# Attention feeding a gated convolution on one core: the keys of the later batches by plain loads summed on VectorE, a new order of the work over a group's four steps, and a new beginning

## The chip, the core and the metric

The kernel runs on one core of a Trainium2 chip. TensorE (PE), VectorE (DVE), ScalarE (ACT) and GpSimd (POOL) compute; SyncE (SP) computes nothing, it issues transfers (DMAs), one after the other, in the order of the program. POOL can issue transfers of its own. All of them are carried by the core's 16 DMA engines. The metric is the device time of one execution in microseconds (us), smaller being better.

## The reference: what is computed

For each of 4 batches: 12288 queries of 128 channels; keys that are also the values, which are a 4 x 4 mean over a 384 x 32 grid, 768 keys, times a matrix; softmax attention; then a causal convolution over 5 positions as a gate, and two projections.

```python
kv_pool = kv.reshape(B, H // r, r, W // r, r, C).mean(axis=(2, 4))   # r = 4
k = v = kv_pool.reshape(B, -1, C) @ w_sr
s = scale * (q @ k.transpose(0, 2, 1))
a = np.exp(s - s.max(-1, keepdims=True))
a /= a.sum(-1, keepdims=True) + 1e-09
x = a @ v
# then, over the sequence, K = 5, xp = x with 4 zeros ahead:
gate_pre = sum(conv_w[k] * xp[:, k:k + S] for k in range(K))
out = ((1 / (1 + exp(-gate_pre))) * (x @ w_val)) @ w_out
```

## The kernel before

**Groups and steps.** Queries are worked in 96 groups of 512 (24 per batch), each in four *steps* of 128 queries, numbered j = 0 to 3. The loop over t = 4 x group + step writes out by hand, engine by engine, what is issued in each step; every engine takes its instructions in that order. Work on a group is spread over six groups' time: `cur` is the group whose scores are being exponentiated, `last`, `avg`, `xg`, `mg`, `og` are those 1, 2, 3, 4 and 5 groups back.

**A tile of scores.** `score` (L262) makes 128 x 768 scores for the next step, as three sums of high and low parts. There are three such score tiles in PSUM, two banks each; a tile is free again when `p_lo` has read it. `row_max` (L268, DVE), `expo` (L280, ACT, in place), `p_hi` (L327, ACT) and, one step later, `p_lo` (L331, DVE) turn it into a high and a low half in f16, in `hl`.

**The transposes.** The weights `hl` of two steps together go through one transposing DMA (L335) into `pt`. In step 2 it is issued for steps 0 and 1 (in this text the *early* transpose), in step 0 of the next group for steps 2 and 3 (the *late* one). Two groups later, `av` (L344) multiplies `pt` with the values in 18 matmuls of 512 columns, split over the four steps by `AV_CUTS` (6, 3, 3 and 6 of them), into one PSUM bank. Each needs both transposes.

**The sums of the softmax.** The reciprocal of the sums (L287, step 0) is turned by PE (L290) into the shared bank `m`, copied (L297, step 1), written to DRAM as `rd` (L298) and read back broadcast to 128 partitions as `rb` (L303, step 3).

**After the attention.** In step 3, `x` (L361, DVE) is `av` times `rb`. Then POOL makes the taps and sums of the convolution (L371, L380; the last tap on ACT, L369), PE the two projections (`m`, L400 and L410), with tanh, product and evacuation between them; `out` leaves in pairs of groups (L424).

**Transfers on SP**, in order, for a pair of groups: q of two groups (L233, 512 KB), late transpose, `out` (512 KB), rd, early transpose, `rb` (256 KB), late transpose, rd, early transpose, `rb`. q is loaded two groups ahead.

**The keys.** For the first batch they come in 16 pieces of 384 KB (L118), each summed by DVE over 4 x 4 (L123). For the other three, `setup_steps` issues one thing per group, from the second group of the batch before: row 0 of each half of the grid by a plain load on SP (L131, 768 KB), then rows 1, 2, 3, each added onto it in SBUF by an accumulating DMA from POOL (L133, 768 KB, one in every second group); then 4 sums over 4 neighbours on DVE (L138), the projection (L150), and the values (L193). Six small instructions ahead of the values and 14 conversions of the weights of the gate (L89, L93, L96) are spread out by `drip`.

`on_pe(j)`, j >= NX, would send a step's tile through PE instead of the transposing DMA; with NX = 4 it holds for none.

Of the kernel before, what the change touches and what calls it, by code (L numbers as in the profile page):

```python
# [15 lines left out]
R = 4  # L16
# [11 lines left out]
def attn_moe_kernel(ctx, tc, qT, kvT, w_sr, w_moe, outT):  # L28
# [12 lines left out]
    AV_CUTS = (0, 6, 9, 12, 18)  # L41
    assert 3 * NCH == AV_CUTS[-1]
    PC = NK // PIECES
    QC = NK // 4
# [3 lines left out]
    kvp = ctx.enter_context(tc.tile_pool(name="kvp", bufs=4))  # L48
# [3 lines left out]
    pfp = ctx.enter_context(tc.tile_pool(name="pfp", bufs=3))  # L52
# [21 lines left out]
    def load_moe():  # L74
# [4 lines left out]
        raw = kvp.tile([C, HALF * R], F32, name="rows0", bufs=1).bitcast(I32)[:, :2 * NW]  # L79
        rest = kvp.tile([C, HALF * R], F32, name="rows1", bufs=1)  # L80
# [34 lines left out]
    def load_kv(st, i):  # L115
        t = kvp.tile([C, R, PC * R], F32, name="kvt", bufs=5)
        src = kvT[0].rearrange("r c x -> c r x")
        nc.sync.dma_start(out=t, in_=src[:, :, i * PC * R:(i + 1) * PC * R])  # L118
        st["kv", i] = t

    def pool_kv(st, i):
        t = st.pop(("kv", i))
        nc.vector.tensor_reduce(out=st["pool"][:, i * PC:(i + 1) * PC],  # L123
                                in_=t.rearrange("c r (k s) -> c k r s", s=R),
                                axis=AX.XY, op=ALU.add)

    def load_rows(b, st, h, r):
        src = kvT[b, r, :, h * HALF * R:(h + 1) * HALF * R]
        if r == 0:
            st["rows", h] = kvp.tile([C, HALF * R], F32, name=f"rows{h}", bufs=1)  # L130
            nc.sync.dma_start(out=st["rows", h], in_=src)  # L131
        else:
            nc.gpsimd.dma_start(out=st["rows", h], in_=src, accum_op=ALU.add)  # L133

    def pool_rows(st, i):
        t = st["rows", i // 2].rearrange("c (k s) -> c k s", s=R)
        k0 = i % 2 * QC
        nc.vector.tensor_reduce(out=st["pool"][:, i * QC:(i + 1) * QC], in_=t[:, k0:k0 + QC],  # L138
                                axis=AX.X, op=ALU.add)
# [116 lines left out]
    def score(g, j):  # L256
# [7 lines left out]
        g.s[j] = s[:, :, :HALF]  # L264

# [5 lines left out]
    def on_pe(j):  # L271

        return j >= NX

    def expo(g, j):
        if j == 0:
            g.z = zs[g.i % len(zs)]
        if on_pe(j):
            g.pf[j] = pfp.tile([P, NK], F32, name="pf")
        nc.scalar.activation(out=halves(g.pf[j]) if on_pe(j) else g.s[j], in_=g.s[j],  # L280
                             func=AF.Exp, bias=g.nm.pop(j), accum_out=g.z[:, j:j + 1])
# [23 lines left out]
    def turn(g, j):  # L305

        pf = g.pf.pop(j)
        for k in range(NCH):
            c = k % (NCH // 2) * P
# [136 lines left out]
    for i in range(5):  # L446
        load_kv(st, i)
# [182 lines left out]
```

## Time and profile before

| | |
|---|---|
| runs of the kernel, us | 1245.61, 1246.01, 1255.13; median 1246.01 |
| profiled execution, span | 1239.7 us from the first to the last instruction |
| beside the span | 1246.01 - 1239.7 = 6.3 us, if that execution is like the median one |
| busiest engines | PE 84%, ACT 73%, DVE 72%, POOL 71% of the span |
| DMA engines | 253.21 MB, mean 204 GB/s; busy 0.9 and more in nearly every slice |

The profiled execution is one of its own; its whole time is not told, only its span. A row of the timeline has the start in us, the duration, engine, line, operation, output<-input, the shapes, a count, and in brackets the idle time before it with what ended it. A row of an SP transfer gives the time for which SP was at issuing it, not that of its landing. In the rows of groups a busy time and a mean in ns stand behind the bar. The source view of a line gives least/median/greatest duration in ns and the first and last start in us.

### The profile page before, as it was taken

Reading aid. Unit: us, or ns where it says so; the run is one execution under the profiler, and the core shown is the slowest. Engines: PE = TensorE matmul, PEld = TensorE weight load, DVE = VectorE, ACT = ScalarE, POOL = GpSimd, SP = SyncE. Lnnn points to the kernel's source line nnn. Section 1 sums busy time; section 2 is a strip of 40 time slices with the busy share of each in tenths; the row PEclk is TensorE's granted clock in tenths of the full one; section 3 lists DMA queues with packets and bytes.
Section 4 is the critical chain, followed back from the end, with each engine's and each line's share of the span. In section 5 each row is a group of like instructions: output and inputs, shape, how many; then the busy total and the mean of one; then the engine's idle time right before and its main releaser. Section 6 shows DMA issues by size and latency. Waiting matters only on the chain.

```text
span 1239.7 us, 15458 instructions
## 1 busy us (share of the span) xinstructions
PE 1039.8 (84%) x4598; PEld 674.5 (54%) x4598; DVE 892.6 (72%) x1254; ACT 899.1 (73%) x1659; POOL 878.3 (71%) x966
## 2 busy tenths in 40 slices
PE   2888778699998768779999778769999999899996
PEld 1655445466565445445666545446566666566663
DVE  6966656588886657568888556557888888787784
ACT  1867666588887557668888657656888888788882
POOL 1277667678886668667888667657788888788782
PEclk9989889899999888889999988888999999999998
DMA  7799999999999999999999999999999999999994
GB/s 248 146 217 179 218 192 214 177 213 204 211 219 209 215 174 216 194 182 225 211 225 232 172 192 218 181 169 217 222 211 217 217 213 226 203 230 212 208 221 119
DMA packets 637235, 253.21 MB, mean 204 GB/s; under 512 B 600160, under 2 KB 609120, under 8 KB 637152
## 3 DMA queue, kind: packets, MB, share of 16 engines
q1 hardware_dynamic: 634560, 238.07, 94.8%
q0 software_dynamic: 2592, 14.16, 8.6%
q8 instruction: 37, 0.61, 0.2%
q14 instruction: 46, 0.38, 0.1%
HBM read 75.83 MB, written 25.36 MB: 82 GB/s over the span
## 4 chain that ended last, share of the span: by engine, by line
PE 43%; DMA 28%; DVE 13%; ACT 9%; issue 5%; POOL 1%; SPq 0%; DVEq 0%; ACTq 0%; POOLq 0%
DMA pt<-hl 23%; PE av L344 17%; PE s L262 16%; PE m L400 5%; ACT s L280 4%; DVE nm L268 4%; PE m L410 3%; DVE x L361 3%; DMA rb<-rd 3%; DVE hl L331 3%; ACT hl L327 2%; DMA kvt<-in_kv 1%; DMA q<-in_q 1%; DVE h L405 1%; ACT th L396 1%
## 5 line engine op out<-in xcount | busy, mean ns | idle before, releaser
L344 PE MATMUL av<-pt,vh 128*128 128x512 f16 x1140 | 420.2, 397 | 134.1 <-DMA pt<-hl 102.5
L280 ACT ACTIVATE s<-s,nm 128x768 f32<-128x768 f32 x384 | 335.6, 874 | 257.5 <-DVE z L287 146.4
L331 DVE SCALAR_TENSOR_TENSOR hl<-s,hl 128x768 f16<-128x768 f32 x384 | 363.0, 945 | 25.1 <-ACT hl L327 24.8
L380 POOL TENSOR_TENSOR sum<-sum,tap 128x512 f32<-128x512 f32 x282 | 359.9, 1276 | 26.4 <-ACT tap L369 4.4
L268 DVE TENSOR_REDUCE nm<-s 128x1 f32<-128x768 f32 x384 | 364.3, 949 | 2.6 <-PE s L262 2.6
L371 POOL TENSOR_SCALAR tap<-x,wm 128x512 f32<-128x512 f32 x376 | 253.6, 696 | 149.2 <-DVE x L361 146.9
L327 ACT ACTIVATE hl<-s 128x768 f16<-128x768 f32 x384 | 310.6, 809 | 18.4 <-issue 6.6
L344 PEld LDWEIGHTS <-vh 128*128 128x128 f16 x1164 | 116.5, 100 | 315.2 <-issue 192.2
L262 PE MATMUL s<-kh,qh 128*128 128x384 f32 x768 | 267.0, 430 | 21.2 <-DVE hl L331 15.5
L248 POOL TENSOR_TENSOR ql<-q,qh 128x512 fp32r<-128x512 f32 x96 | 121.6, 1267 | 163.8 <-ACT qh L244 154.1
L344 PE MATMUL av<-pt,vl 128*128 128x512 f16 x570 | 226.2, 397 | 0.0
L262 PE MATMUL s<-kl,qh 128*128 128x384 f32 x768 | 201.6, 344 | 0.0
L361 DVE SCALAR_TENSOR_TENSOR x<-av,down,rb 128x512 f32<-128x512 f32 x95 | 71.3, 751 | 180.1 <-DMA rb<-rd 89.8
L262 PE MATMUL s<-kh,ql 128*128 128x384 f32 x768 | 200.3, 342 | 0.0
L262 PEld LDWEIGHTS s<-kh,qh 128*128 128x128 f32 x768 | 142.9, 199 | 85.3 <-PE m L290 28.0
L262 PEld LDWEIGHTS s<-kl,qh 128*128 128x128 f32 x768 | 144.6, 195 | 0.5 <-DVE kl L163 0.5
L262 PEld LDWEIGHTS s<-kh,ql 128*128 128x128 f32 x768 | 143.3, 193 | 0.0
L380 POOL TENSOR_TENSOR sum<-tap,tap 128x512 f32<-128x512 f32 x94 | 119.8, 1275 | 0.0
L405 DVE SCALAR_TENSOR_TENSOR h<-th,m 128x512 f32<-128x512 f32 x94 | 64.7, 688 | 68.0 <-PE m L400 51.7
L344 PEld LDWEIGHTS <-vl 128*128 128x128 f16 x582 | 58.2, 100 | 88.4 <-issue 67.7
L400 PE MATMUL m<-x,wm 128*128 128x512 f32 x188 | 100.0, 614 | 5.5 <-DVE r L297 5.5
L410 PE MATMUL m<-h,wm 128*128 128x512 f32 x188 | 96.9, 596 | 3.9 <-DVE h L405 3.9
(62 smaller groups left out, 639.9 us busy)
## 6 DMA issues: line engine op xcount, KB each, us to landing
rb<-rd SPq DMA_DIRECT2D x96, 256.0 KB, 3.7
q<-in_q SPq DMA_DIRECT2D x47, 512.0 KB, 5.6
out<-o SPq DMA_DIRECT2D x46, 512.0 KB, 3.8
rows<-in_kv POOLq DMA_DIRECT2D x18, 768.0 KB, 14.5
kvt<-in_kv SPq DMA_DIRECT2D x16, 384.0 KB, 5.7
rows<-in_kv SPq DMA_DIRECT2D x6, 768.0 KB
pt<-hl SPq DMA_TRANSPOSE x192, 6.1
rd<-r SPq DMA_DIRECT2D x96, 2.0 KB
```

What stands on the lines that cost most here:

```text
L248: nc.gpsimd.tensor_tensor(out=g.ql, in0=g.q, in1=g.qh.bitcast(F32), op=ALU.subtract)
L262: nc.tensor.matmul(s[:, h, :HALF], a[:, sl], k[:, h * HALF:(h + 1) * HALF], start=(i == 0), stop=(i == 2))
L268: nc.vector.tensor_reduce(out=nm, in_=g.s[j], axis=AX.XY, op=ALU.max, negate=True)
L280: nc.scalar.activation(out=halves(g.pf[j]) if on_pe(j) else g.s[j], in_=g.s[j], func=AF.Exp, bias=g.nm.pop(j), accum_out=g.z[:, j:j + 1])
L327: nc.scalar.activation(out=part(g, j, 0), in_=g.s[j], func=AF.Copy, scale=2.0 ** 15)
L331: nc.vector.scalar_tensor_tensor(out=part(g, j, 1), in0=g.s.pop(j), scalar=2.0 ** 15, in1=part(g, j, 0), op0=ALU.mult, op1=ALU.subtract)
L344: nc.tensor.matmul(out, g.st[v][:, k * P:(k + 1) * P], g.pt[:, j0:j1, a * NCH + k], start=(i == 0), stop=(i == len(AV_ORDER) - 1))
L361: nc.vector.scalar_tensor_tensor(out=g.x[:, HALO + c0:HALO + c1], in0=av, scalar=g.st["down"], in1=g.rb[:, c0:c1], op0=ALU.mult, op1=ALU.mult)
L371: eng.tensor_scalar(out=g.tap[k], in0=src, scalar1=w, scalar2=1.0, op0=ALU.mult, op1=ALU.mult)
L380: nc.gpsimd.tensor_tensor(out=s, in0=acc, in1=g.tap[k], op=ALU.add)
L400: nc.tensor.matmul(m, wval, g.x[:, HALO + c0:HALO + c1], start=True, stop=True)
L410: nc.tensor.matmul(m, wout, h, start=True, stop=True)
```

## The change

**Keys.** `load_kv` now serves all batches: in step 1 of groups 1, 3, ... 15 of a batch it loads two pieces of the next batch (768 KB) on SP. In step 1 of groups 3 to 18, DVE sums one piece over 4 x 4. The accumulating DMAs of POOL and the plain loads of rows are gone. Projections stand in step 1 of groups 11 and 19, values in groups 22 and 23. There are three buffers of up to 768 KB.

**Steps.** `x` moves from step 3 to step 0 of the next group, behind the row maximum and `p_lo`; the convolution starts in that step; its last tap and sum stay in step 1. The value projection moves from step 1 to 2, the output projection from step 2 to step 0 of the next group. The turned reciprocals go into 128 spare columns of the next score tile, in step 1, the copy to step 2. `AV_CUTS` becomes 3, 6, 3, 6. q is loaded four groups ahead, with three buffers. The branch `on_pe` and its helpers leave the code.

**Beginning and end.** The first keys come as 1, 1, 2, ..., 2, 1, 1 pieces in three buffers; weights of the gate are loaded after the first scores, and all their conversions go through `drip`, two per step. After the loop, one more output projection and one more `x` stand there.

How this moves the instructions. First SP, in the program of before, where the keys of a later batch begin (rows0 and rows1 are the halves of the grid, pt the transposed weights, hl the untransposed):

```order
L303 DMA rb_3171<-rd_3103 128x512
L233 DMA q_3177<-in_q 128x1024
L335 DMA_TRANSPOSE pt_3142<-hl_3074 128x24x128
L424 DMA out_0<-o_3043 128x1024
L298 DMA rd_3227<-r_3226 4x128
L335 DMA_TRANSPOSE pt_3266<-hl_3197 128x24x128
L303 DMA rb_3296<-rd_3227 128x512
L131 DMA rows0_3304<-in_kv 128x1536
L131 DMA rows1_3306<-in_kv 128x1536
L335 DMA_TRANSPOSE pt_3266<-hl_3197 128x24x128
```

And SP in the changed program, a pair of groups in the second batch that loads keys:

```order
L227 DMA q_3396<-in_q 128x1024
L313 DMA_TRANSPOSE pt_3367<-hl_3295 128x24x128
L407 DMA out_0<-o_3297 128x1024
L287 DMA rd_3475<-r_3474 4x128
L313 DMA_TRANSPOSE pt_3485<-hl_3415 128x24x128
L292 DMA rb_3510<-rd_3475 128x512
L313 DMA_TRANSPOSE pt_3485<-hl_3415 128x24x128
L118 DMA kvt_3577<-in_kv 128x4x384
L287 DMA rd_3593<-r_3592 4x128
L313 DMA_TRANSPOSE pt_3603<-hl_3531 128x24x128
L292 DMA rb_3628<-rd_3593 128x512
```

The order of the others is the same; a key load now stands between the late transpose and rd in every second group, where before two stood once per batch, behind rb.

POOL before, where an accumulating load stands between the copy of x and the taps:

```order
L380 TENSOR_TENSOR sum1_630<-sum0_628,tap4_607 128x512
L248 TENSOR_TENSOR ql_653<-q_563,qh_651 128x512
L357 COPY x_676<-x_558 128x4
L133 DMA rows0_453<-in_kv 128x1536
L371 TENSOR_SCALAR tap0_733<-x_676,wm_108 128x512
```

POOL in the changed program has the same without L133.

DVE before, from step 2 to step 0 of the next group:

```order
L331 SCALAR_TENSOR_TENSOR hl_1051<-s_1034,hl_1051 128x768
L268 TENSOR_REDUCE nm_1138<-s_1102 128x1
L331 SCALAR_TENSOR_TENSOR hl_1051<-s_1061,hl_1051 128x768
L361 SCALAR_TENSOR_TENSOR x_1146<-av_1041,down_222,rb_1030 128x512
L268 TENSOR_REDUCE nm_1166<-s_1125 128x1
L287 RECIPROCAL z2_103<-z2_103 128x4
L331 SCALAR_TENSOR_TENSOR hl_1051<-s_1102,hl_1051 128x768
```

DVE in the changed program, from step 3 to step 1 of the next group:

```order
L263 TENSOR_REDUCE nm_1117<-s_1079 128x1
L309 SCALAR_TENSOR_TENSOR hl_1032<-s_1054,hl_1032 128x768
L388 SCALAR_TENSOR_TENSOR h_1125<-th_1099,m_1089 128x512
L263 TENSOR_REDUCE nm_1144<-s_1104 128x1
L276 RECIPROCAL z2_100<-z2_100 128x4
L309 SCALAR_TENSOR_TENSOR hl_1032<-s_1079,hl_1032 128x768
L339 SCALAR_TENSOR_TENSOR x_1154<-av_1024,down_187,rb_1009 128x512
L263 TENSOR_REDUCE nm_1185<-s_1131 128x1
L309 SCALAR_TENSOR_TENSOR hl_1148<-s_1104,hl_1148 128x768
L123 TENSOR_REDUCE pool_296<-kvt_958 128x48
```

x stood ahead of the row maximum of step 0, and stands behind the low half that follows it; the sum of a key piece (pool) comes in step 1.

The core of the diff:

```diff
-    AV_CUTS = (0, 6, 9, 12, 18)
+    AV_CUTS = (0, 3, 9, 12, 18)
...
-    kvp = ctx.enter_context(tc.tile_pool(name="kvp", bufs=4))
+    kvp = ctx.enter_context(tc.tile_pool(name="kvp", bufs=3))
...
-    def load_kv(st, i):
-        t = kvp.tile([C, R, PC * R], F32, name="kvt", bufs=5)
-        src = kvT[0].rearrange("r c x -> c r x")
-        nc.sync.dma_start(out=t, in_=src[:, :, i * PC * R:(i + 1) * PC * R])
-        st["kv", i] = t
+    def load_kv(b, st, i, n=2):
+
+        t = kvp.tile([C, R, 2 * PC * R], F32, name="kvt")[:, :, :n * PC * R]
+        src = kvT[b].rearrange("r c x -> c r x")
+        nc.sync.dma_start(out=t, in_=src[:, :, i * PC * R:(i + n) * PC * R])
+        for k in range(n):
+            st["kv", i + k] = t[:, :, k * PC * R:(k + 1) * PC * R]
...
     def pool_kv(st, i):
-        t = st.pop(("kv", i))
         nc.vector.tensor_reduce(out=st["pool"][:, i * PC:(i + 1) * PC],
-                                in_=t.rearrange("c r (k s) -> c k r s", s=R),
+                                in_=st.pop(("kv", i)).rearrange("c r (k s) -> c k r s", s=R),
                                 axis=AX.XY, op=ALU.add)
-
-    def load_rows(b, st, h, r):
-        src = kvT[b, r, :, h * HALF * R:(h + 1) * HALF * R]
-        if r == 0:
-            st["rows", h] = kvp.tile([C, HALF * R], F32, name=f"rows{h}", bufs=1)
-            nc.sync.dma_start(out=st["rows", h], in_=src)
-        else:
-            nc.gpsimd.dma_start(out=st["rows", h], in_=src, accum_op=ALU.add)
...
-    def value_steps(st):
-        return [lambda: trickle.extend(column_scale(st)), lambda: None, lambda: None,
-                lambda: values(st, 0, misc()) or split_values(st, 0),
-                lambda: values(st, 1, misc()) or split_values(st, 1)]
-
-    def setup_steps(b, st):
-        loads = [(h, r) for r in range(1, R) for h in range(2)]
-        steps = [lambda: key_tiles(st) or load_rows(b, st, 0, 0) or load_rows(b, st, 1, 0)]
-        for h, r in loads:
-            steps += [lambda: None, lambda h=h, r=r: load_rows(b, st, h, r)]
-        steps += [lambda i=i: (None, lambda: pool_rows(st, i)) for i in range(4)]
-        steps += [lambda h=h: project(st, h, misc()) or split_keys(st, h) for h in range(2)]
-        return steps + value_steps(st)
+    def setup_step(k, b, st):
+
+        if k == 1:
+            key_tiles(st)
+        if k < PIECES and k % 2 == 1:
+            load_kv(b, st, k - 1)
+        if 3 <= k < 3 + PIECES:
+            pool_kv(st, k - 3)
+        if k == 20:
+            trickle.extend(column_scale(st))
+
+    def setup_matmul(k, st):
+        for h, at_k in enumerate((11, 19)):
+            if k == at_k:
+                project(st, h, misc())
+                return split_keys(st, h)
+        for h, at_k in enumerate((22, 23)):
+            if k == at_k:
+                values(st, h, misc())
+                return split_values(st, h)
+        return None, None
...
-        q = io.tile([C, 2, GQ], F32, name="q")
+        q = io.tile([C, 2, GQ], F32, name="q", bufs=3)
...
+        g.spare = s[:, 0, HALF:]
...
-        acc = g.tap[0]
-        for i, k in enumerate(range(1, TAPS)):
-            s = work.tile([C, GQ], F32, name=f"sum{i % 2}", bufs=1 + i % 2)
-            nc.gpsimd.tensor_tensor(out=s, in0=acc, in1=g.tap[k], op=ALU.add)
-            acc = s
-        g.gate = acc
+        g.gate = g.tap[0]
+        for k in range(1, TAPS - 1):
+            g.gate = add_taps(g, g.gate, k)
+
+    def g_conv_last(g):
+        g.gate = add_taps(g, g.gate, TAPS - 1)
...
-    for i in range(5):
-        load_kv(st, i)
-    load_second = load_pair(at(0), at(1), parts=2)
     nc.sync.dma_start(out=wsr, in_=w_sr)
-    g_qh(at(0))
-    g_ql(at(0))
+    loads = [(0, 1), (1, 1)] + [(i, 2) for i in range(2, PIECES - 2, 2)]
+    loads += [(PIECES - 2, 1), (PIECES - 1, 1)]
+    ahead = 3
+    load_second = None
+    for n in range(ahead):
+        load_kv(0, st, *loads[n])
     low = None
     for i in range(PIECES):
-        if i + 5 < PIECES:
-            load_kv(st, i + 5)
-        if i == 3:
-            convert = load_moe()
-        pool_kv(st, i)
-        if i >= 8 and convert:
-            convert.pop(0)()
-        if i == 3 * PIECES // 4:
+        if any(i == first + n - 1 for first, n in loads) and ahead < len(loads):
+            pool_kv(st, i)
+            load_kv(0, st, *loads[ahead])
+            ahead += 1
+            if ahead == len(loads) - 3:
+                load_second = load_pair(at(0), at(1), parts=2)
+        else:
+            pool_kv(st, i)
+        if i == PIECES - 3:
             low()
+        if i == PIECES - 4:
+            g_qh(at(0))
+            g_ql(at(0))
...
+    load_pair(at(2), at(3))
     g_qh(at(1))
     g_ql(at(1))
-
-    steps = value_steps(st)
+    convert = load_moe()
+    trickle += column_scale(st) + convert
...
-        if j == 0 and gi % 2 == 0 and at(gi + 2):
-            load_pair(at(gi + 2), at(gi + 3))
-        if gi % NG == 1 and j == 0 and at(gi + NG - 1):
-            steps += setup_steps(cur.b + 1, states[cur.b + 1])
-        if t == NT + 2:
-            trickle += convert
+        k = gi % NG
+        ahead = states[cur.b + 1] if cur.b + 1 < B else None
+        if j == 0 and gi % 2 == 0 and at(gi + 4):
+            load_pair(at(gi + 4), at(gi + 5))
 
         if nxt:
             score(nxt, (j + 1) % NT)
-        if mg and j == 1:
+        if last and j == 1:
+            norm_turn(last, nxt.spare)
+        if og and j == 0:
+            og.m = g_out(og.h, misc())
+        if gi == 1 and j in (0, 1):
+            values(st, j, misc())
+            high, low = split_values(st, j)
+        if ahead is not None and j == 1 and k > 1:
+            high, low = setup_matmul(k, ahead)
+        if avg:
+            av_slice(avg, AV_CUTS[j], AV_CUTS[j + 1])
+        if mg and j == 2:
             mg.m = g_val(mg, misc())
+
+        if last and j == 2:
+            norm_store(last)
+        row_max(cur, j)
+        if last and j == 0:
+            norm_reciprocal(last)
+        expo(cur, j)
+        p_hi(cur, j)
+        if j == NT - 1:
+            norm_eps(cur)
+            if at(gi + 2):
+                g_qh(at(gi + 2))
+        if og and j == 0:
+            out_tile(og)
+            g_evac(og, og.m)
+        if xg and j == 1:
+            tap(xg, TAPS - 1, nc.scalar)
+            g_conv_last(xg)
         if mg and j == 2:
-            mg.m = g_out(mg.h, misc())
-        if avg:
-            av_part(avg, j)
-
-        if high and (j == 0 or t < NT):
+            mg.th = g_tanh(mg.gate)
+        if high:
             high()
             high = None
-        row_max(cur, j)
-        expo(cur, j)
-        if on_pe(j):
-            turn(cur, j)
-        if j == NT - 1:
-            norm_eps(cur)
-            if mg:
-                out_tile(mg)
-                g_evac(mg, mg.m)
-        p_hi(cur, j)
-        if mg and j == 0:
-            mg.th = g_tanh(mg.gate)
-        if xg and j == 1:
-            tap(xg, TAPS - 1, nc.scalar)
-        if last and j == 0:
-            norm_reciprocal(last)
-        if last and j == 1:
-            norm_store(last)
-        drip()
         if prev:
             p_lo(prev, (j - 1) % NT)
-        if low and (j == 0 or t < NT):
+        if low:
             low()
             low = None
-        if last and j == 0:
-            norm_turn(last, misc())
+        if xg and j == 0:
+            new_x(xg, mg, nc.gpsimd.tensor_copy)
+            g_x(xg, xg.av)
+            g_conv(xg)
+        if mg and j == 3:
+            mg.h = g_h(mg.th, mg.m)
+        if ahead is not None and j == 1:
+            setup_step(k, cur.b + 1, ahead)
         drip()
-        if mg and j == 1:
-            mg.h = g_h(mg.th, mg.m)
-        if avg and j == 3:
-            new_x(avg, xg, nc.gpsimd.tensor_copy)
-            g_x(avg, avg.av)
-        if xg and j == 1:
-            g_conv(xg)
+        drip()
         if last and j == 3:
             norm_rows(last)
-        if at(gi + 2) and j == 2:
-            g_qh(at(gi + 2))
+        if j == NT - 1 and at(gi + 2):
             g_ql(at(gi + 2))
-        if og and j == 0 and og.i % 2:
+        if og and j == 1 and og.i % 2:
             store_pair(og)
-        if steps and (j == 3 or t < NT):
-            high, low = steps.pop(0)() or (None, None)
...
```

More of the change, by code (lines that the diff above doesn't have):

```diff
@@ L51, in attn_moe_kernel @@
     hlp = ctx.enter_context(tc.tile_pool(name="hlp", bufs=2))
-    pfp = ctx.enter_context(tc.tile_pool(name="pfp", bufs=3))
     ptp = ctx.enter_context(tc.tile_pool(name="ptp", bufs=4))
@@ L78, in load_moe @@
             return []
-        raw = kvp.tile([C, HALF * R], F32, name="rows0", bufs=1).bitcast(I32)[:, :2 * NW]
-        rest = kvp.tile([C, HALF * R], F32, name="rows1", bufs=1)
+        raw = kvp.tile([C, R, 2 * PC * R], F32, name="kvt").rearrange("c r x -> c (r x)")
+        raw = raw.bitcast(I32)[:, :2 * NW]
+        rest = kvp.tile([C, R, 2 * PC * R], F32, name="kvt").rearrange("c r x -> c (r x)")
         nc.sync.dma_start(out=raw, in_=w_moe.bitcast(I32))
@@ L269, in row_max @@
         g.nm[j] = nm
-    def on_pe(j):
-        return j >= NX
     def expo(g, j):
@@ L277, in expo @@
             g.z = zs[g.i % len(zs)]
-        if on_pe(j):
-            g.pf[j] = pfp.tile([P, NK], F32, name="pf")
-        nc.scalar.activation(out=halves(g.pf[j]) if on_pe(j) else g.s[j], in_=g.s[j],
+        nc.scalar.activation(out=g.s[j], in_=g.s[j],
                              func=AF.Exp, bias=g.nm.pop(j), accum_out=g.z[:, j:j + 1])
@@ L303, in norm_rows @@
         nc.sync.dma_start(out=g.rb, in_=row.broadcast_to([C, GQ]))
[L305 to L309, printed above, removed]
-            nc.tensor.transpose(g.s[j][:, k // (NCH // 2), c:c + P], pf[:, k * P:(k + 1) * P],
-                                ident)
     def pt_tile(g):
@@ L318, in part @@
     def part(g, j, a):
-        if on_pe(j):
-            return pt_tile(g)[:, j, a * NCH:(a + 1) * NCH].rearrange("p (h k) q -> p h (k q)", h=2)
         if g.hl is None:
@@ L333, in p_lo @@
         if j % 2:
-            j0 = j - 1
+            j0 = j - j % 2
             nc.sync.dma_start_transpose(
@@ L345, in av_range, with av_slice @@
                              start=(i == 0), stop=(i == len(AV_ORDER) - 1))
-    def av_part(g, part):
-        if part == 0:
+    def av_slice(g, lo, hi):
+        if lo == 0:
             g.av = ps_av.tile([C, GQ], F32, name="av")
-        av_range(g, g.av, AV_CUTS[part], AV_CUTS[part + 1])
+        av_range(g, g.av, lo, hi)
     def new_x(g, prev, copy):
@@ L372, in tap, with add_taps @@
                               op0=ALU.mult, op1=ALU.mult)
+    def add_taps(g, acc, k):
+        s = work.tile([C, GQ], F32, name=f"sum{1 - k % 2}", bufs=1 if k % 2 else 2)
+        nc.gpsimd.tensor_tensor(out=s, in0=acc, in1=g.tap[k], op=ALU.add)
+        return s
     def g_conv(g):
@@ L435, in attn_moe_kernel @@
             g.i, g.b, g.t0, g.st = len(groups), b, i * GQ, states[b]
-            g.s, g.nm, g.pf, g.hl, g.pt = {}, {}, {}, None, None
+            g.s, g.nm, g.hl, g.pt = {}, {}, None, None
             groups.append(g)
@@ L556, in attn_moe_kernel @@
     p_lo(n1, NT - 1)
+    n5.m = g_out(n5.h, misc())
+    norm_turn(n1, bank())
+    out_tile(n5)
+    g_evac(n5, n5.m)
     store_pair(n5)
-    norm_turn(n1, misc())
+    new_x(n3, n4, nc.scalar.copy)
+    g_x(n3, n3.av)
+    av_slice(n2, 0, 9)
+    norm_store(n1)
+    norm_rows(n1)
+    g_conv(n3)
+    tap(n3, TAPS - 1, nc.scalar)
+    g_conv_last(n3)
     n4.th = g_tanh(n4.gate)
-    norm_store(n1)
     n4.m = g_val(n4, misc())
-    av_part(n2, 0)
-    norm_rows(n1)
-    tap(n3, TAPS - 1, nc.scalar)
-    g_conv(n3)
+    av_slice(n2, 9, 18)
     h = g_h(n4.th, n4.m)
-    for i in (1, 2, 3):
-        av_part(n2, i)
     new_x(n2, n3, nc.scalar.copy)
```

7 lines of the change are left out of this document (removed).

## The prediction

> **What bounds the kernel now.** I read the page first, then where the groups run fast and where slow, then the queue that carries the transposes.
>
> ```profile
> span 1239.7 us, 15458 instructions
> PE 1039.8 (84%) x4598; PEld 674.5 (54%) x4598; DVE 892.6 (72%) x1254; ACT 899.1 (73%) x1659; POOL 878.3 (71%) x966
> q0 software_dynamic: 2592, 14.16, 8.6%
> rows<-in_kv POOLq DMA_DIRECT2D x18, 768.0 KB, 14.5
> kvt<-in_kv SPq DMA_DIRECT2D x16, 384.0 KB, 5.7
> pt<-hl SPq DMA_TRANSPOSE x192, 6.1
> ```
>
> No engine is full: PE, the busiest, stands at 84%. The span is 1239.7 us and the median of the three runs 1246.01, so 6.3 us lie around the span; I add them at the end. Queue 0 (software) carries only the 18 accumulating loads.
>
> One reciprocal (L287) runs in step 0 of every group but the first, so counting them gives the pace. The source view of L287 in five windows:
>
> ```profile
> L287 DVE RECIPROCAL z<-z x14: 166/167/170, 68.6 to 254.2; 128x4 f32<-128x4 f32 x14
> L287 DVE RECIPROCAL z<-z x8: 166/170/170, 254.2 to 332.1; 128x4 f32<-128x4 f32 x8
> L287 DVE RECIPROCAL z<-z x14: 167/168/170, 376.2 to 562.9; 128x4 f32<-128x4 f32 x14
> L287 DVE RECIPROCAL z<-z x14: 166/168/170, 683.9 to 872.6; 128x4 f32<-128x4 f32 x14
> L287 DVE RECIPROCAL z<-z x24: 166/170/171, 950.5 to 1201.5; 128x4 f32<-128x4 f32 x24
> ```
>
> In the three stretches of 13 intervals each, where the next batch's keys are loaded, a group takes 185.6, 186.7 and 188.7 us over 13: 14.28, 14.36 and 14.52 us. In the last batch, which loads no keys, it takes 251.0/23 = 10.91 us; in between, 77.9/7 = 11.13 us.
>
> What sets 10.91? The timeline of the SP queue, one pair of groups of the last batch:
>
> ```profile
> 995.25 0.37 SPq L233 DMA_DIRECT2D q<-in_q  x1
> 995.67 5.87 SPq L335 DMA_TRANSPOSE pt<-hl  x1
> 1001.59 0.57 SPq L424 DMA_DIRECT2D out<-o  x1
> 1002.26 0.28 SPq L298 DMA_DIRECT2D rd<-r  x1
> 1002.64 4.05 SPq L335 DMA_TRANSPOSE pt<-hl  x1
> 1006.75 0.57 SPq L303 DMA_DIRECT2D rb<-rd  x1
> 1007.42 4.35 SPq L335 DMA_TRANSPOSE pt<-hl  x1
> 1011.86 0.42 SPq L298 DMA_DIRECT2D rd<-r  x1
> 1012.39 3.63 SPq L335 DMA_TRANSPOSE pt<-hl  x1
> 1016.12 0.55 SPq L303 DMA_DIRECT2D rb<-rd  x1
> 1016.76 0.38 SPq L233 DMA_DIRECT2D q<-in_q  x1
> ```
>
> Each instruction starts about 0.1 us after the one before it ended: the queue never waits for data. A transpose is issued in 3.63 us when little lies ahead of it, in 4.35 behind the 256 KB of rb, in 5.87 behind rb and q (768 KB). So what is loaded ahead of a transpose stretches it. From q to q passes 21.51 us, 10.76 per group. That it is late, and not waiting, shows in the engines:
>
> ```profile
> 1002.85 0.75 DVE L361 SCALAR_TENSOR_TENSOR x<-av,down,rb 128x512 f32<-128x512 f32 x1 [1.07 <-POOL ql L248]
> 1004.47 0.93 DVE L331 SCALAR_TENSOR_TENSOR hl<-s,hl 128x768 f16<-128x768 f32 x1
> 1005.54 0.58 PE L262 MATMUL s<-kh,qh 128*128 128x384 f32 x2 [0.32 <-DVE hl L331]
> 1013.33 0.75 DVE L361 SCALAR_TENSOR_TENSOR x<-av,down,rb 128x512 f32<-128x512 f32 x1 [1.08 <-POOL x L357]
> ```
>
> The low half that completes tiles 2 and 3 is written at 1005.40; its transpose starts at 1007.42, two microseconds later, because the queue was still at the one before. I take the queue as the bound, with PE close behind it. Two consecutive x rows (1002.85 and 1013.33) are 10.48 us apart, with 0.32 us of PE wait for a low half, so PE alone needs some 10.17 us per group.
>
> In the slow stretches an accumulating load takes the engines away from that queue. Timeline, and busy time by window (the last two columns are DMA share and GB/s):
>
> ```profile
> 226.04 12.49 SPq L335 DMA_TRANSPOSE pt<-hl  x1
> 237.97 0.75 DVE L361 SCALAR_TENSOR_TENSOR x<-av,down,rb 128x512 f32<-128x512 f32 x1 [8.44 <-DMA rb<-rd]
> 225.00:237.00 12.00, 6.55 (x32) 4.47 (x30) 4.24 (x5) 6.08 (x12) 5.23 (x5) 0.98 1.19 107
> 10.00:24.00 14.00, 1.65 (x2) 0.50 (x2) 11.19 (x18) 1.49 (x3) 1.26 (x1) 1.00 1.09 334
> ```
>
> A transpose is held 12.49 us, rb lands so late that DVE stands 8.44 us, and the engines, fully busy, move 107 GB/s where plain loads of the beginning move 334.
>
> **The change part by part.** *The accumulating loads go.* Without them the 39 intervals fall to the pace of the last batch: 185.6 + 186.7 + 188.7 − 39 × 10.91 = 135.5 us. That is an upper value: it also removes the plain row-0 loads, which come back in another form.
>
> *24 plain loads of 768 KB come onto the SP queue*, each in step 1 of an odd group, behind the late transpose (tiles 2, 3) and ahead of rd and the early one (tiles 0, 1). The nearest rows are the plain row-0 loads, two of 768 KB in a row:
>
> ```profile
> 368.60 0.86 SPq L131 DMA_DIRECT2D rows<-in_kv  x2
> 369.54 8.17 SPq L335 DMA_TRANSPOSE pt<-hl  x1
> ```
>
> Behind rb and both, the transpose took 8.17 us against 4.35 behind rb alone: (8.17 − 4.35 + 0.86)/2 = 2.34 us per load. Other rows bound it: rb and q, as many bytes, cost 5.87 − 3.63 + 0.37 = 2.61; out, a store of 512 KB, 0.57 + 4.05 − 3.63 = 0.99, by size 1.5; at 334 GB/s its 786,432 bytes take 2.35 and its issue about 0.4, 2.8. I take 2.5, near the two loads and q, which read HBM as it does: 24 × 2.5 = 60 us, between 36 and 67. Less than nothing is excluded: the queue gets an instruction it did not have.
>
> The Trainium skill (DMA: Bandwidth & Descriptors, "Issuing engines are not separate DMA queues") speaks against a gain from the queue alone: DMAs from any engine share the same 16 DMA engines and interleave. By it only engine time counts: 8.6% of 1239.7 us is 106.6 us for 18 accumulating loads, 5.9 each, against 2.35 plain, so 64 us saved, 1182 us; the trace agrees that the software load starves the transposes, and the sum below does not use this.
>
> *VectorE sums.* The groups by line, busy time and mean ns; the two PE rows serve a rival below.
>
> ```profile
> L123 DVE TENSOR_REDUCE pool<-kvt 128x48 f32<-128x768 f32 x16 | 15.2, 952 | 7.6 <-DMA kvt<-in_kv 7.4
> L138 DVE TENSOR_REDUCE pool<-rows 128x192 f32<-128x768 f32 x12 | 11.3, 943 | 0.0
> L89 DVE TENSOR_SCALAR rows<-rows 128x261 int32<-128x261 int32 (+1 forms) x6 | 1.7, 284 | 0.0
> L193 PE MATMUL m<-diag,vt 128*128 128x128 f32 x48 | 7.3, 287 | 2.4 <-ACT o L420 2.4
> L150 PE MATMUL m<-pool,wsr 128*128 128x384 f32 x12 | 5.5, 538 | 1.3 <-ACT o L420 1.3
> ```
>
> For each of three batches 16 sums of 0.952 us replace 4 of 0.943: 45.7 − 11.3 = 34.4 us more on DVE. DVE has 892.6 of 1239.7; with 34.4 more it would be busy 927 of some 1160, 80%. Each sum stands in step 1, and I cost it at nothing while the queue's pace (10.9 to 12.2 us) exceeds DVE's 9.3 + 0.95 per group; if that cover goes, at most 34.4 us.
>
> *The new order.* x moves from step 3 to step 0 of the next group, behind the row maximum and the low half; so the 1.08 us for which DVE stands before x (put down to POOL in that row; the last av matmul ends there as well) go, and the late low half is ready some 1.8 us sooner (1.08 and the 0.75 of x). The single av bank is now freed by x in step 0, where PE first does the scores and the output matmul. q is loaded four groups ahead instead of two. The reciprocal transpose leaves the shared bank for the spare columns of a score bank. All this feeds the queue earlier; the queue being late already, I count zero, at most the 0.32 us of PE per group, 91 × 0.32 = 29 us, if PE is the bound. That "all tiles stay on the DMA queue" changes nothing: they do already.
>
> *The beginning.* The 261 KB of weights leave the front of the keys, 0.8 us at 334 GB/s; 8 conversions of 0.284 us or somewhat more (about 2.4 us) go from there, where DVE waits for loads, into the first groups. Three buffers of up to 768 KB stand for five of 384: I take zero, ±2. The end gets one more output matmul and one x, beside the last transposes: +2, from 0 to 4.
>
> **The sum**, on the profiled execution. The start to the fourth reciprocal, 68.6; 91 intervals from 68.6 to 1201.5 at 10.91, 992.8; the end from 1201.5, 38.2: 1099.6. Plus 60 for the loads, plus 2: 1161.6. Plus 6.3: **1168 us**, 6% less. Its own range: pace 10.76 and 36 us, 1130; pace 11.13 and 67 us, 1195.
>
> **The rivals.** *PE sets the pace*: the long transposes only fill time in which SP would wait, and the order frees DVE. With 10.17 to 10.49, say 10.3: 68.6 + 937 + 38.2, at most 12.8 for the values and projections (L193 and L150 above), 6.3: about 1063. For it: PE is near the pace already. Against: the two microseconds of lateness above. *The loads are hidden* in gaps of the DMA engines, and cost their issue, some 0.5: 1099.6 + 12 + 2 + 6.3 = 1120. For it, out is partly hidden; against, q is not. *A new wait:* rd now stands behind the keys in the rings, and rb waits for it on SP:
>
> ```profile
> SPq L303 <- DMA rd<-r: 2.1, 1, 2.1
> ```
>
> It happened once, for 2.1 us; at each of 24 loads it adds 50: 1218. Against: 3.6 us or more of transpose lie between. *Slower than before:* the transpose behind a load waits for its landing, not for its bytes. A 384 KB piece landed in 5.7, twice that is 11.4, less one transpose of 3.63 under it, 7.8 per load, 187 in all, 1295 us. It turns to a loss from (1246.0 − 1107.9)/24 = 5.8 us per load. For it: one queue, and that the accumulating loads landed in 14.5 us. Against: two plain loads together held a transpose by 3.8. *The change misses the cause:* the slow stretches come from the bytes, not the accumulating; then about 1246.
>
> **How the numbers follow.** Queue-bound with visible loads 0.64; PE sets the pace 0.12; loads hidden 0.08; rd behind the keys 0.10; slower 0.04; cause missed 0.02. Prediction 1168. The range reaches over the hidden loads and to rd's case, 1110 to 1220, leaving out PE's pace and the two dear cases, 0.18. A measurement of this kernel tells about 1% from no change. Faster by over 1%: 0.94; within 1%: 0.02; slower: 0.04.
>
> **What would show it.** In the new profile queue 0 is empty and no transpose takes over 9 us; SP is back to back again; the early transpose behind a key load takes 5.4 to 6.2 us, not 3.63; groups with key loads run at 11.8 to 12.4 us, those without at 10.8 to 11.1. If SP shows waits for low halves and the groups run at 10.2 to 10.5, PE had the pace and I am too high; if transposes behind keys take over 8, or rb waits for rd, too low.

## The result, and the profile after

The kernel after takes 1163.47 us (median of 4 runs, 1159.68 to 1166.39) against 1245.81 us before (4 runs, 1233.85 to 1255.13): a ratio of 0.9391, 95% interval 0.9336 to 0.9447. Ratios here and below are of fast runs alone, so they are not always the quotient of the two medians (0.934 here). The forecast was 1168. A second set of six runs on another chip gave 1161.59 us and 0.9372 (0.9327 to 0.9418).

The page of the kernel after, its span, engines, main DMA queue and key loads:

```profile
span 1160.7 us, 15606 instructions
PE 1015.5 (87%) x4598; PEld 674.4 (58%) x4598; DVE 921.8 (79%) x1290; ACT 890.8 (77%) x1660; POOL 866.5 (75%) x947
q1 hardware_dynamic: 643200, 252.23, 103.1%
kvt<-in_kv SPq DMA_DIRECT2D x30, 768.0 KB
```

The software queue 0 is gone, DVE has 29.2 us more (921.8 against 892.6) and the span is 79 us shorter. Only 1.8 us lie around this span (1162.52 for the profiled execution).

The pace, from the source view of the reciprocal, L276 here: a batch that loads keys, the groups behind it, the same again, and the last batch.

```profile
L276 DVE RECIPROCAL z<-z x17: 166/168/178, 309.0 to 501.5; 128x4 f32<-128x4 f32 x17
L276 DVE RECIPROCAL z<-z x8: 160/172/178, 501.5 to 580.1; 128x4 f32<-128x4 f32 x8
L276 DVE RECIPROCAL z<-z x17: 166/178/180, 591.4 to 779.0; 128x4 f32<-128x4 f32 x17
L276 DVE RECIPROCAL z<-z x8: 164/168/180, 779.0 to 859.6; 128x4 f32<-128x4 f32 x8
L276 DVE RECIPROCAL z<-z x24: 166/168/178, 870.9 to 1119.3; 128x4 f32<-128x4 f32 x24
```

While keys are loaded a group takes 192.5/16 = 12.03 and 187.6/16 = 11.73 us, behind that 11.23 and 11.51, in the last batch 248.4/23 = 10.80. Before, the slow stretches ran at 14.3 to 14.5 and the last batch at 10.91. The gain is where the accumulating loads were.

The timeline of SP in after, a pair of groups with a key load (L118) at its end:

```profile
643.00 0.54 SPq L292 DMA_DIRECT2D rb<-rd  x1
643.59 0.41 SPq L227 DMA_DIRECT2D q<-in_q  x1
644.11 5.95 SPq L313 DMA_TRANSPOSE pt<-hl  x1
650.15 0.53 SPq L407 DMA_DIRECT2D out<-o  x1
650.78 0.29 SPq L287 DMA_DIRECT2D rd<-r  x1
651.17 4.18 SPq L313 DMA_TRANSPOSE pt<-hl  x1
655.40 0.58 SPq L292 DMA_DIRECT2D rb<-rd  x1
656.09 4.22 SPq L313 DMA_TRANSPOSE pt<-hl  x1
660.36 0.57 SPq L118 DMA_DIRECT2D kvt<-in_kv  x1
661.03 0.36 SPq L287 DMA_DIRECT2D rd<-r  x1
661.50 4.85 SPq L313 DMA_TRANSPOSE pt<-hl  x1
```

The queue is back to back again. The key load costs its own 0.57 us and makes the early transpose 4.85 us long. Adding up the SP rows from the start of the first transpose to the end of the last gives this account of both kernels (one execution each):

| us on SP | before | after |
|---|---|---|
| first to last transpose | 1180.8 | 1102.8 |
| in the 192 transposes | 981.5 | 905.0 |
| in the other DMAs' issues | 150.7 | 145.2 |
| gaps of over 0.2 us between two rows | 9.1 | 8.0 |
| shorter gaps, some 0.1 us each | 39.5 | 44.6 |

76.5 of the 78.0 us that this stretch lost were lost by the transposes themselves. The same rows of after, grouped by what stands ahead of a transpose since the one before it (without the first two), give these means:

| ahead of it | number | mean us |
|---|---|---|
| rd | 26 | 3.77 |
| out, rd | 45 | 4.32 |
| rb | 50 | 4.36 |
| kvt, rd | 24 | 5.05 |
| rb, q | 45 | 5.91 |

The waits that the rivals spoke of, in the view of waits of after (us in total, times, longest):

```profile
PE av L322 <- DMA pt<-hl: 88.3, 43, 4.5
DVE x L339 <- DMA rb<-rd: 5.2, 4, 2.8
SPq L292 <- DMA rd<-r: 2.1, 1, 2.1
```

PE waits for transposes. rb still waited for rd once, for 2.1 us, not at each key load.

### The profile page after: what moved, and what is told of

The parts are those of the page before. It is cut to its first block, busy times and chain, and to the rows that moved or that the text cites. A ratio compares the mean times of both kernels' runs of the same rounds, so it can differ in the third digit from the quotient of the medians.

```text
span 1160.7 us, 15606 instructions
## 1 busy us (share of the span) xinstructions
PE 1015.5 (87%) x4598; PEld 674.4 (58%) x4598; DVE 921.8 (79%) x1290; ACT 890.8 (77%) x1660; POOL 866.5 (75%) x947
## 5 line engine op out<-in xcount | busy, mean ns | idle before, releaser
L322 PE MATMUL av<-pt,vh 128*128 128x512 f16 x1140 | 414.4, 391 | 97.6 <-DMA pt<-hl 88.3
L256 PE MATMUL s<-kh,qh 128*128 128x384 f32 x768 | 292.0, 462 | 11.9 <-DVE hl L309 10.4
L322 PE MATMUL av<-pt,vl 128*128 128x512 f16 x570 | 222.3, 390 | 0.0
L256 PEld LDWEIGHTS s<-kh,qh 128*128 128x128 f32 x768 | 148.9, 196 | 105.2 <-issue 33.7
L383 PE MATMUL m<-x,wm 128*128 128x512 f32 x188 | 96.0, 592 | 0.0
L269 ACT ACTIVATION_READ_ACCUMULATOR s<-s,nm 128x1 f32 x384 | 76.8, 200 | 0.0
```

The lines of the kernel that those rows point to most:

```text
L256: nc.tensor.matmul(s[:, h, :HALF], a[:, sl], k[:, h * HALF:(h + 1) * HALF], start=(i == 0), stop=(i == 2))
L269: nc.scalar.activation(out=g.s[j], in_=g.s[j], func=AF.Exp, bias=g.nm.pop(j), accum_out=g.z[:, j:j + 1])
L322: nc.tensor.matmul(out, g.st[v][:, k * P:(k + 1) * P], g.pt[:, j0:j1, a * NCH + k], start=(i == 0), stop=(i == len(AV_ORDER) - 1))
L383: nc.tensor.matmul(m, wval, g.x[:, HALO + c0:HALO + c1], start=True, stop=True)
```

## The experiments

The theory: the SP queue with its transposes sets the pace, what stands ahead of a transpose lengthens it, and the gain is that of the accumulating loads. The rivals: the new order carries the gain; PE sets the pace; VectorE's sums or the DMA engines' time decide. The experiments ran on three chips, on which the kernel before took 1237.99, 1238.09 and 1241.75 us; each ratio is to before on the same chip. The kernel after has two sets of runs, 1163.47 us and, on the third of these chips, 1161.59 us. A difference from after, or between kernels of different chips, is therefore uncertain by a few us.

**The old order with plain loads.** In the kernel before:

```
-        loads = [(h, r) for r in range(1, R) for h in range(2)]
-        steps = [lambda: key_tiles(st) or load_rows(b, st, 0, 0) or load_rows(b, st, 1, 0)]
-        for h, r in loads:
-            steps += [lambda: None, lambda h=h, r=r: load_rows(b, st, h, r)]
-        steps += [lambda i=i: (None, lambda: pool_rows(st, i)) for i in range(4)]
+        steps = [lambda: key_tiles(st) or load_two(b, st, 0)]
+        for i in range(PIECES):
+            steps += [lambda i=i: i % 2 and i + 1 < PIECES and load_two(b, st, i + 1)
+                      or (None, lambda: pool_kv(st, i))]
```

(load_two is load_kv of after, on SP, with two buffers of 768 KB in place of three.)

> The kernel before, with its order, its beginning and its end, only the later keys by eight plain loads of 768 KB a batch on the SP queue and 16 VectorE sums a batch. If the accumulating loads alone were the cost and the order is worth nothing, the whole change is here: about 1163 us, 1155 to 1175. If the new order carries a part of the gain (up to the 29 us that I put as its bound), 1180 to 1195. If the order carries the gain, 1210 or more.

Measured: 1183.47 us (1182.54 to 1186.44), ratio 0.9567 (0.9519 to 0.9615). 54.5 us of the gain are in the loads alone; the 20 that are left to after's 1163.47 seemed to be in the order. SP's timeline of this run:

```profile
84.93 0.54 SPq L310 DMA_DIRECT2D rb<-rd  x1
85.52 0.42 SPq L139 DMA_DIRECT2D rows<-in_kv  x1
86.04 6.43 SPq L342 DMA_TRANSPOSE pt<-hl  x1
```

Here the key load stands behind rb, and the transpose behind both takes 6.43 us in this row, 6.86 in the mean of 24. Behind rb alone it is 4.36: a load costs 6.86 + 0.47 (its issue) - 4.36 = 2.97 us. In after it stands ahead of rd, and costs 5.05 + 0.57 - 3.77 = 1.85. That made the place a new suspect.

**The new order with accumulating loads.** In the kernel after:

```
-        if k < PIECES and k % 2 == 1:
-            load_kv(b, st, k - 1)
-        if 3 <= k < 3 + PIECES:
-            pool_kv(st, k - 3)
+            load_rows(b, st, 0, 0)
+            load_rows(b, st, 1, 0)
+        if 3 <= k < 15 and k % 2 == 1:
+            load_rows(b, st, (k - 3) // 2 % 2, 1 + (k - 3) // 4)
+        if 14 <= k < 18:
+            pool_rows(st, k - 14)
```

(load_rows and pool_rows are those of before; the step is taken in step 3 and the projections in groups 18 and 19.)

> The kernel after with its new order, beginning and end, but the later keys again by two plain and six accumulating loads a batch. If the accumulating loads are the cost: as slow as before, 1230 to 1250 us. If the order carries a part: 1200 to 1225. If it carries the gain: below 1180.

Measured: 1199.15 us (1195.26 to 1207.48), ratio 0.9694 (0.9636 to 0.9752). My expectation fell: even with the accumulating loads the kernel is 39 us faster than before. The issues of this run:

```profile
kvt<-in_kv POOLq DMA_DIRECT2D x18, 768.0 KB, 10.4
```

The same loads land in 10.4 us instead of 14.5. In before they lengthen transposes behind rb (46 with a mean of 6.40 us), here those behind rd alone (50 with a mean of 4.36) and, less, those behind rb and q (6.29). So what an accumulating load costs also depends on the work beside it. That the place does it here too was not tried apart.

**No later key loads.** In after:

```
-        if k < PIECES and k % 2 == 1:
-            load_kv(b, st, k - 1)
         if 3 <= k < 3 + PIECES:
+            if not kept:
+                kept.append(const.tile([C, R, PC * R], F32, name="kept"))
+                nc.sync.dma_start(out=kept[0],
+                                  in_=kvT[1].rearrange("r c x -> c r x")[:, :, :PC * R])
+            st["kv", k - 3] = kept[0]
             pool_kv(st, k - 3)
```

> The kernel after without the 24 later key loads: one piece is loaded once and every later sum reads it, so the keys of batches 1 to 3 are not those of the input; sums, projections and all else stay. If the SP queue sets the pace and each load is paid there in full: 24 x 2.0 (its 0.57 us of issue and the 1.4 us by which the transpose behind it is longer in the trace of after) to 24 x 2.5 us less, 1103 to 1115 us. If PE sets the pace and the loads fill waiting time: 1145 to 1163 us.

Measured: 1121.80 us (1121.27 to 1122.67), ratio 0.9061 (0.9024 to 0.9098): 41.7 us less than the first set of after, 39.8 less than the second, 1.7 us per load. Its L280 is the reciprocal, and the last row is the first sum over the one piece that it keeps:

```profile
span 1119.5 us, 15605 instructions
L280 DVE RECIPROCAL z<-z x92: 160/168/181, 78.3 to 1078.5; 128x4 f32<-128x4 f32 x92
72.10 0.95 DVE L123 TENSOR_REDUCE pool<-kept 128x48 f32<-128x768 f32 x1 [7.35 <-DMA kept<-in_kv]
```

Without loads the 91 intervals take 1000.2 us, 10.99 each, the start 78.3 and the end 41.0. The run has a wait of its own: the kept piece is loaded just ahead of its first sum, and DVE stands 7.35 us for it. The kernel after has no wait of DVE there, and its fourth reciprocal comes at 72.0:

```profile
L276 DVE RECIPROCAL z<-z x92: 160/168/180, 72.0 to 1119.3; 128x4 f32<-128x4 f32 x92
```

How much of the 7.35 us was made up later is not known. By the spans the loads thus cost 41.2 (1160.7 - 1119.5) to 48.6 us, 1.7 to 2.0 each. The SP rows lie between: transposes take 875.3 us here and 905.0 in after, the other issues 129.2 and 145.2, together 45.7 or 1.9 per load. Loads are visible on the queue, but cheaper than the 2.5 us that I took.

**Key loads issued by ScalarE.** `load_kv(b, st, k - 1, eng=nc.scalar)` for the later batches.

> The kernel after with the 24 later key loads issued by ScalarE, so that they stand in another queue than the transposes. If it is the place in the SP queue that costs (the transpose behind the load and the load's issue): up to 24 x 2.0 us less, 1115 to 1130 us. If the DMA engines' time costs, whichever queue it comes from: 1155 to 1175 us. If the load, running beside transposes, starves them as the accumulating loads did: above 1180.

Measured: 1152.37 us (1151.43 to 1153.02), ratio 0.9307 (0.9269 to 0.9345). The page of this run has a queue of their own for them:

```profile
q10 hardware_dynamic: 12672, 18.88, 5.5%
kvt<-in_kv ACTq DMA_DIRECT2D x24, 768.0 KB
```

The time lies just under the range that I gave to the DMA engines' time. 9 to 11 of the 40 to 42 us go; at least 30.6 stay (1152.37 - 1121.80, one chip). Off SP the load's issue is gone, but transposes still grow: the 50 behind rb now take 4.99 us in the mean against 4.36, and all together 910.7 us, 35.4 more than without loads. So some three quarters of a load's price stay when it stands in another queue, which fits time of the DMA engines that both queues share. The Trainium skill (DMA: Bandwidth & Descriptors, "Issuing engines are not separate DMA queues") says that transfers of any issuing engine run on the same 16 DMA engines, and that issuing from several saves only the time of the issue. The trace agrees in the main: what goes is no more than the 16.0 us of issue (145.2 - 129.2) that SP is rid of without the loads.

**Key loads behind rb.** In after, each load goes from ahead of rd (odd groups) to behind rb (even groups); sums and projections follow one group later:

```
+        if ahead is not None and j == 3 and k <= PIECES and k > 0 and k % 2 == 0:
+            load_kv(cur.b + 1, ahead, k - 2)
```

> The kernel after, only each later key load moved on the SP queue from ahead of rd and the early transpose (odd groups) to behind rb and ahead of the late transpose (even groups), where the first run has it. If the place of the load makes what the new order is worth: a load cost 6.86 + 0.47 - 4.36 = 2.97 us there and costs 5.05 + 0.57 - 3.66 = 1.96 here, so 24 x 1.0 us more, 1187 us, 1178 to 1195. If the order is worth its 20 us by something else (x and the low half earlier, q four groups ahead): as after, 1158 to 1168.

Measured: 1191.26 us (1187.08 to 1191.51), ratio 0.9624 (0.9546 to 0.9702), against 0.9372 to 0.9391 of after. The place costs 28 to 30 us. SP's timeline:

```profile
165.75 0.58 SPq L290 DMA_DIRECT2D rb<-rd  x1
166.38 0.42 SPq L118 DMA_DIRECT2D kvt<-in_kv  x1
166.90 6.77 SPq L311 DMA_TRANSPOSE pt<-hl  x1
```

The transposes behind rb and a key load are at 6.98 us again (mean of 24).

**The old order, key loads ahead of rd.** The first run of this section, its loads moved:

```
+        if cur.b + 1 < B and j == 1 and gi % NG < PIECES and gi % 2 == 1:
+            if gi % NG == 1:
+                key_tiles(states[cur.b + 1])
+            load_two(cur.b + 1, states[cur.b + 1], gi % NG - 1)
         if last and j == 1:
             norm_store(last)
```

> The first run (the kernel before, with plain later loads), only its 24 key loads moved to step 1 of the odd groups, ahead of rd and the early transpose. If the place is all: 1183 less 24 x 1.0 us, 1159, between 1152 and 1168. If the rest of the new order is worth the 20 us: as that run, 1177 to 1188.

Measured: 1152.23 us (1151.30 to 1155.13), ratio 0.9323 (0.9232 to 0.9414). 31 us better than behind rb (1183.47, another chip). SP's timeline:

```profile
161.43 0.53 SPq L139 DMA_DIRECT2D rows<-in_kv  x1
162.06 0.36 SPq L304 DMA_DIRECT2D rd<-r  x1
162.52 5.13 SPq L341 DMA_TRANSPOSE pt<-hl  x1
```

So the 20 us that seemed to be in the order are in the place that it gives to the key load. At equal places the old order is ahead: 1152.2 against 1161.6 to 1163.5 here, 1183.5 against 1191.3 behind rb, and 1143.3 against 1151.9 with q moved (below). All three say 8 to 11 us. No pair stands on one chip, and the intervals of each pair's ratios touch; single runs overlap in none.

**Halved transposes.** In after, each transpose covers one tile; the `pt` buffers are filled with zeros once (not shown):

```
-                out=pt_tile(g)[:, j0:j + 1].rearrange("p j k q -> p (j k) q"),
-                in_=g.hl[:, j0:j + 1].rearrange("p j a k -> p (j a k)"))
+                out=pt_tile(g)[:, j0:j0 + 1].rearrange("p j k q -> p (j k) q"),
+                in_=g.hl[:, j0:j0 + 1].rearrange("p j a k -> p (j a k)"))
```

> The kernel after with every transpose of one tile instead of two (tiles 1 and 3 stay zeros in their buffers, so half of the weights are left out; matmuls and all else stay). The queue loses about half of 192 x 4.6 us, some 440 us, and can't bind any more. What is left is the other engines' floor: if PE's row of before is right (10.2 us per group), 1035 to 1070 us, the value that the PE rival gave (1063); if something beside both the transposes and PE holds the groups (the softmax chain from score to low half), it stays above 1100.

Measured: 1053.48 us (2 runs alone, 1053.01 and 1053.95), ratio 0.8518 (0.8410 to 0.8626); two runs leave the size uncertain, but both lie over 170 us below the fastest run of before. SP's timeline and, below it, the busy time from the first to the last of 17 reciprocals of the last batch (window, length, PE, PEld, DVE, ACT, POOL, clock, DMA share, GB/s), then the same for the 24 of after:

```profile
998.59 1.44 SPq L318 DMA_TRANSPOSE pt<-hl  x1
1000.12 0.86 SPq L292 DMA_DIRECT2D rb<-rd  x1
1002.10 1.55 SPq L318 DMA_TRANSPOSE pt<-hl  x1
```

```profile
864.90:1023.20 158.30, 158.30 (x750) 107.20 (x748) 138.31 (x193) 147.78 (x271) 145.47 (x159) 1.00 0.73 153
870.90:1119.30 248.40, 231.77 (x1077) 153.98 (x1076) 203.10 (x277) 208.47 (x391) 211.68 (x231) 0.99 1.06 214
```

PE is busy for 158.30 of 158.30 us, 158.3/16 = 9.89 per group: with the transposes halved PE is the bound. In after it isn't: the transposes are, by 110 us. But the run relieves two things at once: SP, and the DMA engines, whose share falls from 1.06 to 0.73. It shows that the transposes bind, not whether SP's issuing itself is too slow or the engines behind it hold SP back. The run with loads from ScalarE speaks for the engines; a run that parts the two for the transposes themselves was not made.

**q ahead of rd.** In after, for groups without key loads:

```
+        if j == 1 and gi % 2 == 1 and not key_group and at(gi + 3):
+            load_pair(at(gi + 3), at(gi + 4))
```

> The kernel after, only q moved, for the 24 or so pairs whose groups carry no key load, from behind rb (transposes there take 5.91 us against 4.36 behind rb alone) to the odd group's place ahead of rd, where that group's transpose has nothing ahead (3.66). If the first bytes ahead of a transpose are cheaper than further ones: it gives back 1.55 and costs 0.6 to 0.95 (out, as many bytes, 0.56 to 0.66; a key load 1.39 for one and a half times as many), so 14 to 24 us less, 1140 to 1150 us. If a byte costs the same anywhere: as after, 1158 to 1168. If PE is what holds these groups: the same.

Measured: 1151.94 us (1150.10 to 1158.25), ratio 0.9323 (0.9244 to 0.9403). SP's timeline:

```profile
992.58 0.53 SPq L227 DMA_DIRECT2D q<-in_q  x1
993.20 0.28 SPq L287 DMA_DIRECT2D rd<-r  x1
993.59 4.64 SPq L313 DMA_TRANSPOSE pt<-hl  x1
```

22 transposes behind q and rd take 4.85 us in the mean, 1.1 more than behind rd (4.85 - 3.77 = 1.08); behind rb the same q costs 5.91 - 4.36 = 1.55. The first bytes ahead of a transpose are the cheaper ones. 22 x (1.55 - 1.08) gives 10 us, and 9.7 to 11.5 were measured against the two sets of after, on other chips and with intervals that touch; the transposes add up to 894.5 us, 10.5 less than in after. That is less than the 14 to 24 that I expected: I had taken q's price there from out, a store, and it is nearly that of a key load.

**The sums twice.** In after, `pool_kv` called twice for every later piece.

> The kernel after with each of the 48 later sums done twice (the second writes the same numbers): 48 x 0.952 = 45.7 us more on VectorE. If the queue hides the sums as I costed them: as after, at most 5 us more. If VectorE's work lies on the path: up to 46 us more, 1185 to 1209.

Measured: 1161.49 us (1152.88 to 1166.83) against 1161.59 of after on the same chip. In the groups by line of this run:

```profile
L123 DVE TENSOR_REDUCE pool<-kvt 128x48 f32<-128x768 f32 x112 | 105.5, 947 | 10.3 <-DMA kvt<-in_kv 8.6
```

48 more sums, 45 us of VectorE, and no time beyond the noise of these runs (some 9 us): they lie beside the queue.

**After again, and two versions that may be better.** after_again is the kernel after. old_order_both_moved is the old order with plain key loads ahead of rd and q moved as above. act_keys_q_ahead is the kernel after with

```
+        if ahead is not None and j == 3 and 1 <= k <= PIECES:
+            load_kv(cur.b + 1, ahead, k - 1, n=1, eng=nc.scalar)
...
+        if j == 1 and gi % 2 == 1 and at(gi + 5):
+            load_pair(at(gi + 5), at(gi + 6))
```

in place of the loads of after.

> The kernel after unchanged, to stand on the same chip beside the next ones and to compare with the old order with its key loads ahead of rd (1152 in the call before). If that order with its beginning and end is really the better one by some 11 us: 1160 to 1167 here. If the 11 us were a difference of chips or calls: 1150 to 1156.

> The old order with its key loads ahead of rd (1152 us) and q moved ahead of rd, too, for the groups without key loads (a third q buffer). If what the two moves give adds up: 22 transposes behind rb at 4.36 instead of 5.91, and 22 behind q and rd at 4.85 instead of 3.66, 22 x 0.36 = 8 us, 1144, between 1138 and 1150. If PE, at 10 us or so a group, holds the groups without key loads by then: 1150 to 1156.

> The kernel after with the later keys in loads of 384 KB, one a group in groups 1 to 16, issued by ScalarE in step 3, and with every q load but the first ones ahead of rd in the odd groups. Both pieces gave some 11 us each alone (keys from ScalarE 1152, q moved 1152). If they add up: 1138 to 1145. If the DMA engines' time sets a floor under them: 1148 to 1155.

Measured on one chip:

| kernel | us | range | ratio to before, 95% |
|---|---|---|---|
| after_again | 1161.59 | 1156.71 to 1171.31 | 0.9372, 0.9327 to 0.9418 |
| old_order_both_moved | 1143.33 | 1142.31 to 1144.46 | 0.9219, 0.9184 to 0.9254 |
| act_keys_q_ahead | 1133.84 | 1129.38 to 1140.64 | 0.9153, 0.9110 to 0.9196 |

Both moves add up in the old order (1152 to 1143). The last version is 27.8 us faster than after, more than the 20 us or so of its two pieces (its key loads are halved as well, which was not tried alone), and beats both kernels. Its page:

```profile
span 1131.0 us, 15670 instructions
PE 1004.0 (89%) x4598; PEld 666.8 (59%) x4598; DVE 920.5 (81%) x1290; ACT 888.8 (79%) x1660; POOL 865.2 (76%) x947
```

## Why the prediction was right, point by point

**The bound: right.** In after, SP has 8.0 us of gaps over 0.2 us between the first and the last transpose, and halving the transposes' bytes takes 110 us away. Whether SP or the DMA engines behind it are the narrower of the two is open, as said above. PE's own pace, which I read as 10.17 us, is 9.89 where it alone binds; the rival's time, 1063, is near the 1053 of that run.

**The sum: right by two errors that cancel, which is luck.** The forecast of the span was 1161.6, and it is 1160.7. But the run without key loads is the sum's base, and its span is 1119.5, where I had 1099.6 + 2 = 1101.6: 17.9 too little. Its start to the fourth reciprocal is 78.3, not 68.6, its 91 intervals 10.99, not 10.91, and its end 41.0, not 40.2. Up to 7.35 us of the start are the wait that only this run has, so the base was 11 to 18 us too small. In the pace I had let every group run at the last batch's pace; the groups behind the key loads, which carry the projection and values of the next batch, don't (11.23 and 11.51 in after, and 11.13 before, a row that I had quoted and not used). Against that the loads cost 41.2 to 48.6 us, not 60: 11 to 19 too much.

**The step that failed: the price of a load.** "The nearest rows are the plain row-0 loads", and 2.5 us, came from transposes behind rb. The load's new place, ahead of rd, was in my text, but I priced it as if the place didn't matter. Where rb stands ahead too, the loads cost 1191.26 - 1121.80 = 69.5 us, 2.9 each; ahead of rd 1.7 by the same reckoning (each up to 0.3 more, for the wait of the run without loads). The early transpose behind a key load has a median of 4.89 us, not the 5.4 to 6.2 that I named.

**The new order at zero: wrong in both directions.** I counted what it does to VectorE and PE, and nothing for the place that it gives to the key load, which is worth 28 to 31 us. At equal places the order, with its beginning, its end and its third key buffer, is 8 to 11 us slower, as far as runs on different chips tell. Some 3 of these are the end: 1160.7 - 1119.3 = 41.4 us from the 95th reciprocal, against 38.2 before, where I had added 2. The rest isn't settled. One row may bear on it, the same window of a key batch in after and in the old order with key loads ahead of rd (columns as above):

```profile
309.00:485.00 176.00, 158.36 (x702) 104.95 (x701) 140.93 (x194) 139.03 (x256) 137.10 (x150) 0.94 1.09 225
```

```profile
309.00:485.00 176.00, 155.00 (x711) 99.70 (x710) 141.33 (x193) 138.96 (x255) 136.76 (x150) 1.00 1.09 233
```

The new order has the lower granted clock, 0.94 against 1.00, and fewer matmuls done; its transposes add up to 905.0 us, the old order's to 893.4. The lower clock is in every run: 0.956 to 0.969 over the ten runs of after, 0.987 to 0.990 over the four of the old order with these loads. Which of these is cause was not tried.

**The accumulating loads.** That they cost by more than their bytes is right: in the new order they are 36 to 38 us slower than plain ones. The 135.5 us were an upper value, as I said. From before to the old order with plain loads well placed it is 1238.1 - 1152.2 = 86, with the plain loads in.

**VectorE's 34 us at nothing: right**, by the doubled sums, within some 9 us.

**The time around the span: mis-sized.** I added 6.3 us, the distance of one profiled execution from the median of others. 1.8 lie there (1162.52 - 1160.7).

**The rivals.** PE's pace: no, but its time is near that of the run with halved transposes. Hidden loads, 1120: no, though what a load costs lies between that and my value. rd behind the keys: no, one wait of 2.1 us as before. The landing that holds a transpose: no, the longest transpose behind a key load of after took 6.5 us. The cause missed: no. Engine time alone, from which I had worked out 1182, is 19 too high.

## What to carry to other kernels

On a queue that is issued back to back, price a load by its place: look at what already stands ahead of the transfer that it will delay, and put it where that is least. When a change moves work and also reorders it, run each half alone before crediting either: here the order looked like 20 us, and at equal places of the loads it costs some 9. A sum that comes out right to 1 us may hold two errors of over 10 us; one run that leaves the disputed work out shows them, if it brings no wait of its own.

## What was not expected of the hardware

The price of bytes ahead of a transpose grows with what is there. 768 KB of keys add 1.3 us to a transpose that has only rd ahead (5.05 against 3.77), and 2.5 to one behind rb (6.86 against 4.36, in the old order).

Half as many bytes took a transpose behind rd from a median of 3.67 us on SP to 1.44, less than half, and nothing ahead lengthened it much any more (1.61 us in the mean behind rb and q, against 5.91). In that run SP had 518 us of gaps over 0.2 us. That the issue of a whole transpose is held back until the queue has room for it would fit both, but was not tried by itself.

Accumulating loads of the same size landed in 14.5 us in one order of the work and in 10.4 in the other.
